# Causal attention ahead of two expert layers: VectorE makes both parts of head 1's next keys, ScalarE copies K1's probabilities and orders the row factors

## The chip, the cores and the metric

One core of a Trainium2 chip. The time is the device time of one launch in microseconds (us). The engines are TensorE (PE in the rows; PEld is its weight load), VectorE (DVE), ScalarE (ACT), GpSimd (POOL) and SyncE (SP, which issues most DMAs). Each engine works through its own queue in order, and semaphores join them.

## The reference

Three layers follow each other, all in float32:

```python
# attention: 4 batches, 8 heads, 576 positions, head size 64; blocks of 64 positions, causal by block
scores = (1 / 8) * q @ k.T
scores = where(block(row) >= block(column), scores, -1e9)
attn = exp(scores - max(scores))
x = (attn / (attn.sum(-1) + 1e-9)) @ v              # 2304 tokens x 512
# experts: each of 2304 tokens goes to one of 8 experts
e = argmax(x @ w_gate + bias[modality])
x = gate * (relu(x @ w1[e]) @ w2[e])
# last layers
h = x @ w_in                                         # 512 -> 2048
g = where(h >= 1, h, where(h <= -1, 0, (h + 1)**2 / 4))
out = g @ w_out                                      # 2048 -> 512
```

The change touches the attention alone.

## The kernel before

**Pairs and kinds.** The attention goes through 16 pairs of heads (4 batches of 4 pairs), numbered 0 to 15. In a pair the rows of the score matrix are cut into seven pieces, the kinds K0 to K6: K0 is rows 0 to 127 of both heads, K1 rows 128 to 255 of both, K2 and K3 rows 256 to 383 of head 0 and of head 1, K4 and K5 rows 384 to 511 of head 0 and of head 1, K6 the last 64 rows of both. One step does one kind, in the order K3, K1, K0, K4, K2, K6, K5 for the pairs 1 to 14 (pair 0 and pair 15 have orders of their own). Pair 3 lies at about 48 to 60 us, pair 8 at 109 to 122 us, pair 14 at 183 to 197 us.

**A step.** `scores` puts the scores of a kind into PSUM (TensorE; the last matmul, L339, adds the causal mask). `flip` turns, with TensorE, the probabilities of the kind two steps back (L378), and they are copied from PSUM into the tile pT: by ScalarE for the kinds in `ON_ACT` (L389), otherwise by VectorE, but then only behind the maximum of this step (`later`, L524). `soft` takes the maximum of each row (VectorE, L354, L358; K6 L349), and ScalarE makes the exponentials and, with a second short instruction, their sums (L360). In each step a copy on ScalarE stands ahead of the exponentials. The PSUM tiles of scores and of flips have two buffers each; those of a kind are free when its exponentials, or its copies, are done. K6 shares one buffer, two banks, with the turned q and k of the next pair.

**What hangs on the steps.** `PLAN` names what `act` issues ahead of the scores (0), behind them (1) or at the end (2) of a step. In the third step of pair n, at its end: `load_k(n + 1)` ("k"), the weighted values of pair n - 1 (`weigh`, 20 matmuls, L403), and `weigh_first` (4 matmuls, L418, and the copy into xT, L422). At the beginning of the fourth step "low" issues the low parts of the next keys, L490; in its middle the copy of the weighted values into xT, L408 ("store").

**Keys.** `load_k` turns k into the PSUM tile psk (576 columns; the upper 64 partitions are head 1, the lower head 0). VectorE copies the first 128 columns into kT (L292). ScalarE rounds each head's half into kd, 64x576 (L294, two instructions). GpSimd copies each half to the other partitions (L296). In the next step VectorE subtracts kd from psk into kl, for both heads (L490, two instructions), and with that psk is free.

**Row factors.** Behind each second pair `row_sums` inverts the sums of the exponentials (VectorE, L427, L428), and `row_order`, called by `weigh_first`, brings them into the order of the tokens: one or two copies of 16 numbers for each partition (L439) and two copies of 2 (L445), from SBUF to SBUF, on VectorE. `rows` uses them later: it multiplies with them on VectorE (L461, L465), behind matmuls on xT (L455).

In pairs 14 and 15 the first steps of the routing are put in between, up to three small VectorE groups for each step (L667 and on).

Of the kernel before, what the change touches and what calls it, by code (L numbers as in the profile page):

```python
# [11 lines left out]
F32 = mybir.dt.float32  # L12
# [6 lines left out]
ALU = mybir.AluOpType  # L19
# [7 lines left out]
B, H, S, D = 4, 8, 576, 64  # L27
NB = S // 64
NP = H // 2
# [20 lines left out]


ORDER_FIRST, ORDER_LAST, ORDER = (2, 4, 0, 1, 5, 6, 3), (3, 1, 4, 2, 6, 0, 5), (3, 1, 0, 4, 2, 6, 5)
PLAN = {(1, 0): ["rows", "q"], (2, 0): ["sum"], (2, 2): ["k", (0, 5), "first"], (3, 0): ["low"], (3, 1): ["store"],
        (4, 0): ["rows"], (6, 2): ["rows"]}
FROM = 0, 128, 256, 320, 448
LAG = 2
COPY = 4
ON_ACT = (0, 2, 3, 4, 5)


KDUP = 1, 1, 0, 0
# [61 lines left out]
def attention(late, weights, tc, q, k, v, ids, w_gate, mbias, x_dram, dram, ident, tabs):  # L123
# [3 lines left out]
    nc = tc.nc  # L127
# [54 lines left out]
    def turned(dst, x):  # L182
        if x.dtype == F32R:
            nc.tensor.transpose(dst.bitcast(F32R), x, identr)
        else:
            nc.tensor.transpose(dst, x, ident)
# [53 lines left out]
    rt = keep.tile([P, NJ, H], F32, name="rt")  # L240
# [4 lines left out]
    def load_q(n):  # L245
        psq = ps2.tile([P, 1024], F32, tag="big", name=f"psq{n}")
        psq = psq[:, 64:64 + S]
        for t, x in enumerate(FROM):
            turned(psq[:, x:x + P], io_t[n, "q"][:, t, :])
        qa, qb, qf = qas[n % 2], qbs[n % 2], qfs[n % 2]  # L250

        qT = wk.tile([P, 9, 64], F32, tag="qT", name=f"qT{n}", bufs=1)
        nc.scalar.activation(qT, psq.rearrange("p (i t) -> p i t", t=64), AF.Copy, scale=D ** -0.5)
        E = nc.gpsimd if n else nc.vector
        copy = nc.gpsimd.tensor_copy if n else nc.scalar.copy
        halves = [(h, slice(h * 64, h * 64 + 64), slice(64 - h * 64, 128 - h * 64)) for h in range(2)]
        for h, hs, oh in halves:
            copy(qa[hs, h, :7], qT[hs, 2:])
            if not n:
                E.tensor_tensor(qa[oh, h, :7], qT[hs, 2:], qa[hs, h, :7].bitcast(F32), op=ALU.subtract)  # L260
        if n:
            for h, hs, oh in halves:
                E.tensor_tensor(qa[oh, h, :7], qT[hs, 2:], qa[hs, h, :7].bitcast(F32), op=ALU.subtract)
        for h, hs, oh in halves:
            copy(qf[hs, h].rearrange("p (i t) -> p i t", t=64), qT[hs, :2])
        E.tensor_copy(qb[:64, :7], qa[:64, 0, :7])
        E.tensor_copy(qb[64:, 7], qa[64:, 1, 6])
        E.tensor_copy(qb[64:, 8:], qa[64:, 1, :6])
        nc.gpsimd.tensor_copy(qzs[n % 2][:, 64:], qa[:, 1, 6])

    low_k = {}

    def load_k(n):
        if n:
            psk = ps2.tile([P, 1024], F32, tag="big", name=f"psk{n}")[:, 64:64 + S]
            ranges = [(psk, slice(0, S))]
        else:

            pk = [ps2.tile([P, 512], F32, tag="x", name=f"psk{n}_{i}", bufs=2) for i in range(2)]
            ranges = [(pk[0][:, :448], slice(0, 448)), (pk[1][:, :P], slice(448, S))]  # L280
        for t, x in enumerate(FROM):
            if n:
                dst = psk[:, x:x + P]
            else:
                dst = pk[t // 4][:, x % 448:x % 448 + P]
            turned(dst, io_t[n, "k"][:, t, :])
        kT = wk.tile([P, S if n == 0 else P], F32, tag="kT" if n else "kT0", name=f"kT{n}", bufs=2 if n else 1)
        kd = wk.tile([P, 2, S], F32R, tag="kd", name=f"kd{n}")
        kl = wk.tile([P, S], F32R, tag="kl", name=f"kl{n}")
        halves = [(h, slice(h * 64, h * 64 + 64), slice(64 - h * 64, 128 - h * 64)) for h in range(2)]  # L290
        if n:
            nc.vector.tensor_copy(kT, psk[:, :P])  # L292
            for h, hs, oh in halves:
                nc.scalar.copy(kd[hs, h], psk[hs])  # L294
            for h, hs, oh in halves:
                nc.gpsimd.tensor_copy(kd[oh, h], kd[hs, h])  # L296
            low_k[n] = [(kl[hs], psk[hs], kd[hs, h].bitcast(F32)) for h, hs, oh in halves]
        else:
            for a, cs in ranges:
                nc.vector.tensor_copy(kT[:, cs], a)  # L300
            for h, hs, oh in halves:
                for u, dst in enumerate((kd[hs, h], kd[oh, h])):
                    if KDUP[2 * h + u] == 0:
                        for a, cs in ranges:
                            nc.scalar.copy(dst[:, cs], a[hs])
                    else:
                        nc.vector.tensor_copy(dst, kT[hs])
                nc.vector.tensor_tensor(kl[hs], kT[hs], kd[hs, h].bitcast(F32), op=ALU.subtract)
        qk[n] = kT, kd, kl
# [53 lines left out]
    def flip(n, i):  # L363
# [10 lines left out]
        for o, k0, k1 in todo:  # L374
# [10 lines left out]
            else:  # L385
                dst = pTs[n][:, :k1, heads[0], P * j:P * (j + 1)]
                src = pt[:, :m, :]
            if i in ON_ACT:
                nc.scalar.copy(dst, src)  # L389
# [16 lines left out]
    def store_xT(n):  # L406
        b, c = divmod(n, NP)
        nc.scalar.copy(xT[:, c, b % 2 * S + 64:(b % 2 + 1) * S], pxs.pop(n))  # L408

    def weigh_first(n, order=True):  # L410

        b, c = divmod(n, NP)
        if n < B * NP - 1:
            px = ps1.tile([P, 512], F32, tag="pt", name=f"py{n}", bufs=4 - SB)
        else:
            px = ps2.tile([P, 512], F32, tag="x", name=f"py{n}", bufs=2)
        for h in range(2):
            nc.tensor.matmul(px[h * 64:(h + 1) * 64, :64], io_t[n, "v"][:, 0, h * D:(h + 1) * D],  # L418
                             pTs[n][:, 0, h, :64], start=True, stop=True)
        if c % 2 and order:  # L420
            row_order(b, c // 2)
        nc.scalar.copy(xT[:, c, b % 2 * S:b % 2 * S + 64], px[:, :64])  # L422

    def row_sums(b, a):

        r = rinv[:, b, 2 * a:2 * a + 2]
        nc.vector.tensor_scalar(r, ssum[:, b, 2 * a:2 * a + 2], 1e-9, None, op0=ALU.add)  # L427
        nc.vector.reciprocal(r, r)  # L428

    def row_order(b, a):  # L430

        r = rinv[:, b, 2 * a:2 * a + 2]
        j0 = NB * b // 2
        if b % 2 == 0:
            parts = [((0, P), (0, P), j0)]
        else:
            parts = [((64, P), (0, 64), j0), ((0, 64), (64, P), j0 + 1)]
        for (lo, hi), (slo, shi), j in parts:
            nc.vector.tensor_copy(rt[lo:hi, j:j + 4, 4 * a:4 * a + 4].rearrange("p j (c h) -> p c h j", h=2),  # L439
                                  r[slo:shi, :, :8].rearrange("p c (h j) -> p c h j", h=2))  # L440

        lo, hi = 64 * (b % 2), 64 * (b % 2) + 64
        rr = rt[lo:hi, j0 + 4, 4 * a:4 * a + 4].rearrange("p (c h) -> p c h", h=2)
        for h in range(2):
            nc.vector.tensor_copy(rr[:, :, h], r[64 * h:64 * h + 64, :, 8])  # L445

    def rows(j, a, spare=False, xr=None):

# [30 lines left out]
    def act(n, z, at):  # L479

        if n >= B * NP:
            return
        for what in PLAN.get((z, at), ()):
            if what == "q" and n + 1 < B * NP:
                load_q(n + 1)
            elif what == "k" and n + 1 < B * NP:
                load_k(n + 1)
            elif what == "low" and n + 1 in low_k:
                for dst, a, b in low_k.pop(n + 1):
                    nc.vector.tensor_tensor(dst, a, b, op=ALU.subtract)  # L490
            elif what == "rows" and todo:
                done.add(todo[0])
                rows(*todo.pop(0))
            elif n == 0:
                continue
            elif isinstance(what, tuple):
                weigh(n - 1, *what)
            elif what == "sum" and (n - 1) % 2:
                row_sums((n - 1) // NP, (n - 1) % NP // 2)
            elif what == "first":  # L500
                weigh_first(n - 1)
            elif what == "store":
                store_xT(n - 1)
                if (n - 1) % 2:
                    todo.extend((j, (n - 1) % NP // 2) for j in rows_of[(n - 1) // NP])
# [5 lines left out]
    for g in range(len(steps) + LAG):  # L511
        n, z = divmod(g, NK)
# [30 lines left out]
    ps1_ctx.close()  # L543
    tail = Tables()
    tail.pv, tail.ps2 = pv_ctx, ps2_ctx
    tail.row_sums = lambda: (row_sums(B - 1, 1), row_order(B - 1, 1))
    tail.weigh = lambda: weigh(B * NP - 1, 0, 5)
    tail.store_xT = lambda: store_xT(B * NP - 1)
    tail.weigh_first = lambda: weigh_first(B * NP - 1, False)
    tail.rows, tail.left = rows, todo + [(j, 1) for j in rows_of[B - 1]]  # L550
    return tail, routing, early

# [1030 lines left out]
```

## Time and profile before

| | |
|---|---|
| runs shown | 835.45, 835.92, 838.87 us; median 835.92 |
| profiled execution | 830.86 us, span 829.1 us |
| TensorE | 806.4 us busy, 97% of the span |
| VectorE | 590.8 us, 71% |
| ScalarE | 477.1 us, 58% |
| GpSimd | 212.0 us, 26% |
| mean granted TensorE clock | 0.997 |

All views are of the one profiled execution. Busy time is the union of an engine's instructions. A matmul's end is modelled, with the time that it takes through the array, so TensorE can be shown busy while a weight load already waits; a wait shows best in the start of the next instruction. [...]

### The profile page before, as it was taken

Reading aid. Unit: us, or ns where it says so; the run is one execution under the profiler, and the core shown is the slowest. Engines: PE = TensorE matmul, PEld = TensorE weight load, DVE = VectorE, ACT = ScalarE, POOL = GpSimd, SP = SyncE. Lnnn points to the kernel's source line nnn. Section 1 sums busy time; section 2 is a strip of 40 time slices with the busy share of each in tenths; the row PEclk is TensorE's granted clock in tenths of the full one; section 3 lists DMA queues with packets and bytes.
Section 4 is the critical chain, followed back from the end, with each engine's and each line's share of the span. In section 5 each row is a group of like instructions: output and inputs, shape, how many; then the busy total and the mean of one; then the engine's idle time right before and its main releaser. Section 6 shows DMA issues by size and latency. Waiting matters only on the chain. (4 is left out here: it accounts for less than half of the span.)

```text
span 829.1 us, 13988 instructions
## 1 busy us (share of the span) xinstructions
PE 806.4 (97%) x4936; PEld 699.8 (84%) x4936; DVE 590.8 (71%) x1071; ACT 477.1 (58%) x964; POOL 212.0 (26%) x313
## 2 busy tenths in 40 slices
PE   6999999998999999999999999999999999999998
PEld 5777777776788888888888999999999988888887
DVE  6777787778756646697873766666636888887784
ACT  4877877776533335455544766766657644444442
POOL 8546556646315414140201000000000011112120
PEclk9999999999999999999999999999999999999999
DMA  7565565532736547665624553554634643333301
GB/s 158 125 163 141 143 166 160 143 81 71 248 80 124 189 135 244 221 203 168 198 87 125 179 174 127 173 176 138 218 130 155 239 149 127 128 127 126 132 35 39
DMA packets 140988, 123.21 MB, mean 149 GB/s; under 512 B 73111, under 2 KB 125351, under 8 KB 138224
## 3 DMA queue, kind: packets, MB, share of 16 engines
q1 hardware_dynamic: 134576, 107.99, 42.9%
q0 software_dynamic: 4992, 13.94, 4.8%
q8 instruction: 41, 0.67, 0.3%
q10 hardware_dynamic: 1344, 0.33, 0.2%
q14 instruction: 35, 0.29, 0.1%
HBM read 89.18 MB, written 40.38 MB: 156 GB/s over the span
## 5 line engine op out<-in xcount | busy, mean ns | idle before, releaser
L1018 PE MATMUL h<-yhi,wi 128*128 128x384 f32 x768 | 199.1, 337 | 1.1 <-ACTq L1257 1.1
L1018 PEld LDWEIGHTS h<-yhi,wi 128*128 128x128 f32 x768 | 138.9, 188 | 1.6 <-ACTq L1257 1.6
L1018 PE MATMUL h<-ylo,wi 128*128 128x384 f32 x384 | 128.7, 335 | 0.0
L1482 POOL DMA_INDIRECT out_dram<-rest,tab x16 | 27.4, 1711 | 336.5 <-DVE rest L1449 331.6
L360 ACT ACTIVATE pall<-s,nmax 128x384 f32<-128x384 f32 (+2 forms) x144 | 79.6, 562 | 35.0 <-DVE nmax L358 29.8
L1297 ACT ACTIVATE cl<-h,half 128x384 f32<-128x384 f32 x96 | 55.8, 581 | 65.1 <-PE h L1018 62.7
L1301 DVE SCALAR_TENSOR_TENSOR gg<-cl,h 128x384 f32<-128x384 f32 x96 | 52.2, 551 | 49.4 <-ACT cl L1298 48.6
L1427 PE MATMUL p<-wo,s 128*128 128x256 f32 (+1 forms) x432 | 87.0, 337 | 0.0
L1427 PEld LDWEIGHTS p<-wo,s 128*128 128x128 f32 x432 | 67.6, 188 | 9.2
L378 PE MATMUL pt<-ident,pall 128*128 128x128 f32 x400 | 65.9, 283 | 6.7 <-ACT pall L360 4.7
L1018 PEld LDWEIGHTS h<-ylo,wi 128*128 128x128 f32 x384 | 72.1, 188 | 0.0
L1427 PE MATMUL p<-wo,a 128*128 128x256 f32 (+1 forms) x330 | 65.4, 334 | 0.0
L1018 PE MATMUL h<-xhi,wh 128*128 128x512 f32 (+2 forms) x164 | 63.7, 388 | 0.0
L1018 PE MATMUL h<-xlo,wh 128*128 128x512 f32 (+2 forms) x164 | 62.1, 379 | 0.4 <-DVE xlo L76 0.4
L1018 PE MATMUL h<-xhi,wl 128*128 128x512 f32 (+2 forms) x164 | 62.2, 379 | 0.4 <-DVE wl L1104 0.2
L1129 PE MATMUL acc<-wh,hl 128*128 128x512 f32 x152 | 59.6, 392 | 0.8 <-DVE hl L1118 0.8
L1129 PE MATMUL acc<-wh,hh 128*128 128x512 f32 x152 | 59.6, 392 | 0.0
L1129 PE MATMUL acc<-wl,hh 128*128 128x512 f32 x152 | 59.4, 391 | 0.0
L1427 PEld LDWEIGHTS p<-wo,a 128*128 128x128 f32 x330 | 52.2, 188 | 8.0
L1298 ACT ACTIVATE cl<-cl 128x384 f32<-128x384 f32 x96 | 50.5, 526 | 3.0
L378 PEld LDWEIGHTS pt<-ident,pall 128*128 128x128 f32 x400 | 43.1, 142 | 10.4 <-ACT pall L360 8.3
L1101 ACT CAST wh<-raw 128x1024 fp32r<-128x1024 f32 x40 | 41.8, 1047 | 15.7 <-PE acc L1129 15.7
(312 smaller groups left out, 1774.2 us busy)
## 6 DMA issues: line engine op xcount, KB each, us to landing
raw<-in_moe_w_dram SPq DMA_DIRECT2D x80, 256.0 KB, 3.5
g_dram<-gg SPq DMA_DIRECT2D x48, 384.0 KB, 2.6
g<-g_dram SPq DMA_DIRECT2D x18, 1024.0 KB, 4.9
wi_raw<-in_moe_w_in_dram SPq DMA_DIRECT2D x16, 512.0 KB, 4.7
wo_raw<-in_moe_w_out_dram SPq DMA_DIRECT2D x16, 512.0 KB, 4.0
yr<-y_dram SPq DMA_DIRECT2D x18, 256.0 KB, 4.6
x_dram<-xrow SPq DMA_DIRECT2D x34, 128.0 KB, 2.2
v<-in_v_dram SPq DMA_DIRECT2D x32, 128.0 KB, 2.4
```

The source lines that it names most:

```text
L360: nc.scalar.activation(pall[n % 2][:, o:o + w], pss[:, u:u + w], AF.Exp, bias=nm[:, x:x + 1], scale=1.0, accum_out=ssum[:, b, c, x:x + 1])
L378: nc.tensor.transpose(pt[:, kk, :], pa[:, o + kk * P:o + (kk + 1) * P], ident)
L1018: nc.tensor.matmul(ps, a[za], b[zb], start=(i == 0), stop=(i == n - 1))
L1101: nc.scalar.copy(ws[s, f][0], weights.raw[s, f])
L1129: nc.tensor.matmul(accs[s][u], a[:, us], b[:, 1, :], start=(f == 0 and i == 0), stop=(f == NF - 1 and i == 2))
L1297: nc.scalar.activation(cl, ph, AF.Relu, bias=half, scale=0.5)
L1298: nc.scalar.activation(cl, cl, AF.Square)
L1301: nc.vector.scalar_tensor_tensor(gg[:, :, f % 2, :], cl.rearrange(t3, t=P), 1.0, ph.rearrange(t3, t=P), op0=ALU.min, op1=ALU.max)
L1427: nc.tensor.matmul(o, a, b, start=(x == 0 and i in FRESH), stop=(x == len(terms) - 1), skip_group_check=True)
L1482: outs.append(nc.gpsimd.indirect_dma_start(out=out[:, :], out_offset=bass.IndirectOffsetOnAxis(ap=tabs.tab[:, j:j + 1].bitcast(U32), axis= ...
```

## The change

There are three edits. ScalarE copies K1's probabilities too (`ON_ACT`), so of the copies only K6's stay with VectorE. `load_k` gives head 1's kd to VectorE, which makes head 1's low part right behind it, in the third step; head 0's kd stays with ScalarE, and head 0's low part stays at the beginning of the fourth step. `row_order` goes from `weigh_first` to an entry of its own, "order", ahead of "k", and runs on ScalarE; for the last pair it stays on VectorE.

```diff
-PLAN = {..., (2, 2): ["k", (0, 5), "first"], (3, 0): ["low"], ...
+PLAN = {..., (2, 2): ["order", "k", (0, 5), "first"], (3, 0): ["low"], ...
-ON_ACT = (0, 2, 3, 4, 5)
+ON_ACT = (0, 1, 2, 3, 4, 5)
@@ load_k
             nc.vector.tensor_copy(kT, psk[:, :P])
-            for h, hs, oh in halves:
-                nc.scalar.copy(kd[hs, h], psk[hs])
-            for h, hs, oh in halves:
-                nc.gpsimd.tensor_copy(kd[oh, h], kd[hs, h])
-            low_k[n] = [(kl[hs], psk[hs], kd[hs, h].bitcast(F32)) for h, hs, oh in halves]
+            low = [(kl[hs], psk[hs], kd[hs, h].bitcast(F32)) for h, hs, oh in halves]
+            for h, copy in ((1, nc.vector.tensor_copy), (0, nc.scalar.copy)):
+                copy(kd[halves[h][1], h], psk[halves[h][1]])
+                if h:
+                    nc.vector.tensor_tensor(*low[1], op=ALU.subtract)
+                nc.gpsimd.tensor_copy(kd[halves[h][2], h], kd[halves[h][1], h])
+            low_k[n] = low[:1]
@@ weigh_first
-        if c % 2 and order:
-            row_order(b, c // 2)
@@ row_order: each nc.vector.tensor_copy becomes copy
-    def row_order(b, a):
+    def row_order(b, a, copy=nc.scalar.copy):
@@ act
+            elif what == "order":
+                if (n - 1) % 2:
+                    row_order((n - 1) // NP, (n - 1) % NP // 2)
@@ the last pair
-    tail.row_sums = lambda: (row_sums(B - 1, 1), row_order(B - 1, 1))
+    tail.row_sums = lambda: (row_sums(B - 1, 1), row_order(B - 1, 1, nc.vector.tensor_copy))
```

## Rows read from the trace of the kernel before

**Rows 1.** Busy time of a stretch: stretch, length, engines (instructions), PEclk, DMA share, GB/s.
```profile
20.00:190.00 170.00, 163.59 (x1318) 126.75 (x1319) 132.78 (x282) 132.53 (x391) 96.37 (x173) 1.00 0.53 139
```

**Rows 2.** Waits, 20 to 190 us: total, times, longest.
```profile
PEld pt L378 <- ACT pall L360: 7.7, 21, 0.4
```

**Rows 3.** Timeline of pair 3, from its fourth step: start, us, what [idle before].
```profile
53.46 1.52 DVE L490 TENSOR_TENSOR kl<-psk,kd 64x576 fp32r<-64x576 f32 x2 [2.27 <-ACT kd L294]
...
53.76 0.21 ACT L422 COPY xT<-py 128x64 f32<-128x64 f32 x1 [0.34 <-PE py L418]
...
54.22 0.20 PE L339 MATMUL s<-maskk,maskq 128*128 128x64 bf16 x1
...
54.26 0.63 PE L378 MATMUL pt<-ident,pall 128*128 128x128 f32 x4
...
55.02 0.69 DVE L358 TENSOR_REDUCE nmax<-s 128x1 f32<-128x512 f32 x1
...
55.58 0.20 PE L339 MATMUL s<-maskk,maskq 128*128 128x64 bf16 x1
...
55.62 0.68 DVE L524 COPY pT<-pt 128x512 f32<-128x512 f32 x1
55.74 0.69 ACT L360 ACTIVATE pall<-s,nmax 128x512 f32<-128x512 f32 x1 [1.28 <-DVE nmax L358]
...
56.42 0.36 ACT L389 COPY pT<-pt 128x256 f32<-128x256 f32 x1
...
56.66 0.60 PE L378 MATMUL pt<-ident,pall 128*128 128x128 f32 x4
...
56.77 0.55 DVE L358 TENSOR_REDUCE nmax<-s 128x1 f32<-128x384 f32 x1
...
57.35 0.58 ACT L360 ACTIVATE pall<-s,nmax 128x384 f32<-128x384 f32 x1 [0.57 <-DVE nmax L358]
...
57.58 0.20 PE L339 MATMUL s<-maskk,maskq 128*128 128x64 bf16 x1
...
58.08 0.31 PEld L378 LDWEIGHTS pt<-ident,pall 128*128 128x128 f32 x3 [0.41 <-ACT pall L360]
...
58.39 0.75 ACT L360 ACTIVATE pall<-s,nmax 128x576 f32<-128x576 f32 x1
...
59.28 0.53 PEld L378 LDWEIGHTS pt<-ident,pall 128*128 128x128 f32 x5 [0.37 <-ACT pall L360]
```

**Rows 4.** Timeline of pair 8, third and fourth step.
```profile
111.47 2.33 POOL L263 TENSOR_TENSOR qa<-qT,qa 64x448 fp32r<-64x448 f32 x2
...
111.60 0.29 DVE L292 COPY kT<-psk 128x128 f32<-128x128 f32 x1 [0.21 <-PE psk L184]
...
111.92 1.92 DVE L439 COPY rt<-rinv 64x16 f32<-64x16 f32 x2
...
112.83 1.29 ACT L294 CAST kd<-psk 64x576 fp32r<-64x576 f32 x2
...
115.90 0.69 DVE L358 TENSOR_REDUCE nmax<-s 128x1 f32<-128x512 f32 x1
```

**Rows 5.** Two lines' own views: duration in ns (shortest/median/longest), first and last start.
```profile
L439 DVE COPY rt<-rinv x12: 174/720/1161, 38.9 to 212.2; 64x16 f32<-64x16 f32 x8, 128x16 f32<-128x16 f32 x4
...
L389 ACT COPY pT<-pt x80: 361/485/587, 16.0 to 212.0; 128x384 f32<-128x384 f32 x32, 128x512 f32<-128x512 f32 x32, 128x256 f32<-128x256 f32 x16
```

**Rows 6.** Pairs 0 and 14: timelines, and the stretch with the lower clock as in rows 1.
```profile
20.04 0.37 PE L326 MATMUL s<-kd,qa 128*128 128x288 f32 x1 [1.79 <-DVE kl L490]
...
188.81 0.28 DVE L292 COPY kT<-psk 128x128 f32<-128x128 f32 x1
...
190.89 0.54 PE L687 MATMUL rkp<-oh,ones 128*128 128x104 bf16 x13 [1.60 <-ACT xT L422]
...
193.54 0.69 PE L378 MATMUL pt<-ident,pall 128*128 128x128 f32 x2 [1.09 <-DVE pT L524]
...
193.00:197.00 4.00, 3.46 (x16) 3.18 (x17) 3.43 (x14) 2.18 (x6) 0.07 (x1) 0.57 0.11 37
```

More of the change, by code (lines that the diff above doesn't have):

```diff
@@ L52 @@
 ORDER_FIRST, ORDER_LAST, ORDER = (2, 4, 0, 1, 5, 6, 3), (3, 1, 4, 2, 6, 0, 5), (3, 1, 0, 4, 2, 6, 5)
-PLAN = {(1, 0): ["rows", "q"], (2, 0): ["sum"], (2, 2): ["k", (0, 5), "first"], (3, 0): ["low"], (3, 1): ["store"],
+PLAN = {(1, 0): ["rows", "q"], (2, 0): ["sum"], (2, 2): ["order", "k", (0, 5), "first"], (3, 0): ["low"], (3, 1): ["store"],
         (4, 0): ["rows"], (6, 2): ["rows"]}
@@ L408, in store_xT, with weigh_first @@
         nc.scalar.copy(xT[:, c, b % 2 * S + 64:(b % 2 + 1) * S], pxs.pop(n))
-    def weigh_first(n, order=True):
+    def weigh_first(n):
         b, c = divmod(n, NP)
@@ L438, in row_order @@
         for (lo, hi), (slo, shi), j in parts:
-            nc.vector.tensor_copy(rt[lo:hi, j:j + 4, 4 * a:4 * a + 4].rearrange("p j (c h) -> p c h j", h=2),
+            copy(rt[lo:hi, j:j + 4, 4 * a:4 * a + 4].rearrange("p j (c h) -> p c h j", h=2),
                                   r[slo:shi, :, :8].rearrange("p c (h j) -> p c h j", h=2))
@@ L444, in row_order @@
         for h in range(2):
-            nc.vector.tensor_copy(rr[:, :, h], r[64 * h:64 * h + 64, :, 8])
+            copy(rr[:, :, h], r[64 * h:64 * h + 64, :, 8])
     def rows(j, a, spare=False, xr=None):
@@ L545, in attention @@
     tail.pv, tail.ps2 = pv_ctx, ps2_ctx
-    tail.row_sums = lambda: (row_sums(B - 1, 1), row_order(B - 1, 1))
+    tail.row_sums = lambda: (row_sums(B - 1, 1), row_order(B - 1, 1, nc.vector.tensor_copy))
     tail.weigh = lambda: weigh(B * NP - 1, 0, 5)
     tail.store_xT = lambda: store_xT(B * NP - 1)
-    tail.weigh_first = lambda: weigh_first(B * NP - 1, False)
+    tail.weigh_first = lambda: weigh_first(B * NP - 1)
     tail.rows, tail.left = rows, todo + [(j, 1) for j in rows_of[B - 1]]
```

## The prediction

> **What bounds the kernel now.** I read the busy time first. Over the span TensorE is busy for 97%, and in the steady part of the attention for 163.59 of 170 us [rows 1]. So time is won only where TensorE stands still, by this view 6.4 us of that stretch. Then the waits: in that stretch TensorE's weight loads for the flips wait 21 times for ScalarE's exponentials, 7.7 us [rows 2]. No other wait of TensorE there repeats.
>
> Then the order in time, for head pair 3 [rows 3]. VectorE stands still 2.27 us for ScalarE's kd copies, and only then makes the two low parts (1.52 us). The maximum of K4 is behind them in its queue and starts at 55.02, though K4's scores had ended at 54.42 (54.22 + 0.20). ScalarE waits 1.28 us for that maximum. VectorE then copies K1's probabilities (0.68) and forms the products of `rows`, so K2's maximum starts at 56.77, and ScalarE waits again, 0.57. Its exponential of K2 begins at 57.35 and TensorE, which wants to flip it behind the mask of 57.58, waits to 58.08. An unhindered flip follows its mask by 0.04 (54.22 to 54.26), so this one costs 0.46, though 0.41 is shown: each shown wait hides about 0.05. A second wait, 0.37, is for K6's exponential, which starts at 58.39 because ScalarE has run without a pause since 57.35. The reader is to see that VectorE is late by about 0.6 to 1 us in each pair, because it idles ahead of that while ScalarE does both kd copies.
>
> **The change part by part.** *Keys.* ScalarE loses one kd copy, 0.64 (1.29 for two [rows 4]). VectorE gains a copy of 64x576 out of PSUM. That row does not exist. From below: 0.29 for the 128x128 one [rows 4]; from above: the subtraction of the same size, 0.76 [rows 3]. The copy of 512 columns takes 0.68 [rows 3], so I take 0.75. It and head 1's subtraction (0.76) fit into the 2.27 us of idling, and head 0's subtraction needs ScalarE's single copy, which is done 0.64 earlier. In pair 3 VectorE would start at 51.2 (53.46 less 2.27), have head 1 done by 52.7, head 0 by 53.5, before K4's scores end at 54.42. K4's maximum starts at 54.46 instead of 55.02. The cover is the TensorE work of `weigh`; without it the copy would cost its 0.75. GpSimd's copies come in the same order, with an input that is ready earlier. No DMA moves.
>
> *K1's copy.* VectorE loses 0.68; ScalarE gains 0.58 [rows 5], ahead of K4's exponential and behind flips that end at 54.89 (54.26 + 0.63). So K4's exponential starts at 55.5 at the latest instead of 55.74: a smaller step than VectorE's. K2's maximum starts when its own scores are done (55.58 + 0.20), near 55.85 instead of 56.77, and ends near 56.4. ScalarE reaches K2's exponential 0.68 after K4's (55.74 to 56.42, the copy) and 0.36 more for that copy, at 56.5. That is 0.85 ahead of 57.35, against a wait of 0.46: the first wait goes, with 0.4 to spare. For K6: TensorE's flips of K4 end near 57.3, ScalarE's copy of them takes 0.5, the exponential 0.75, so it ends near 58.5; TensorE gets there at 58.4 (59.28 less both waits). Of the second wait about 0.15 stays.
>
> *Row factors.* In seven of the pairs VectorE loses four (or three) tiny copies: 1.92 us for the first two in pair 8 [rows 4], beside 0.17 for the shortest of these [rows 5]. They start at 111.92 and end with GpSimd's subtractions (111.47 + 2.33), so they stood still for GpSimd. On ScalarE such a copy has no row. From below 0.17, VectorE's shortest [rows 5]; the nearest row, ScalarE's 64 columns, is 0.21 [rows 3]; from above VectorE's longest, 1.16 [rows 5]. I take 0.21, four make 0.84. They stand ahead of ScalarE's kd copy: 112.83 + 0.84 + 0.64 = 114.31, head 0's subtraction ends at 115.1, and K4's maximum starts near 115.15 instead of 115.90, just when K4's scores are done. What waits behind them on ScalarE is the kd copy and the two xT copies; the first of these needs TensorE's result at 114.46 anyway. So they cost nothing, with 0.2 to spare.
>
> [...]
>
> *The sum.* Pairs 1 to 13: of the 21 waits three (0.9) belong to pair 0, which I keep apart. 18 are left, 6.8 shown and 0.9 hidden, 7.7 in all. From this I take 0.15 for each of the five pairs with a second wait: 7.0. Pair 0: TensorE waits 1.79 for the low part of pair 1's keys [rows 6]; the subtraction ends 0.75 earlier, but K1's copy then lies in a stretch in which ScalarE is full, so between 0 and 0.8, and I take 0.5. [...] VectorE now goes from its key copy at 188.81 to the end of the K1 copy, which releases TensorE at 193.5; with 0.28 + 0.75 + 0.76, a short wait for kd, 0.76 and 0.69 it would be done at 192.2, so 1.2 us earlier. [...] I take 1.8, between 1.0 and 2.9. Sum: 7.0 + 0.5 + 1.8 = 9.3 us.
>
> The profiled execution took 830.86 us (829.1 of span and 1.8 around it), 5.1 below the median of 835.92. So 821.6 by its own measure, and carried to the median **826.6 us**. Nothing behind the attention pays it back: TensorE has its work ready there, and the rest moves up as a whole.
>
> **Rivals.**
> (B) *ScalarE becomes the bound.* For it: it has run without a pause from 57.35 on, and gains 0.58 while it loses 0.64 at another place. Against it: the copy falls into its 1.28 us of waiting. If K2's exponential moves only as far as K4's, by 0.24, the 18 waits give 4.3, pair 0 nothing and pair 14 1.0: 5.3 us, 830.6.
> (C) *VectorE's copy does not run beside GpSimd*, and the change so doesn't do what it says. For it: the row factors stood still until GpSimd's subtractions were over. If the copy too started only then (in the last pairs about 2 us later), head 0's low part would end 0.3 after the one of before, and only the K1 copy that has gone would help: 1 to 3 us, 834. Against it: the key copy, also out of PSUM, started 0.13 us after GpSimd and took 0.29 [rows 4].
> [...]
> (D) *Slower: the row factors on ScalarE.* If one takes p there, K4's maximum of such a pair starts at 114.3 + 4p instead of 115.90; from p = 0.40 on the pair loses. At 1.16 (rows 5) it loses 3.0, seven pairs 21, against some 5 won elsewhere: 852. The whole kernel loses from p = 0.58. Against it: the small ScalarE copy out of PSUM takes 0.21 [rows 3].
> (E) *The clock.* If pair 14's first wait stays (ScalarE now has four small copies ahead of it and one kd copy less, 0.2 more in all) and the clock falls as before, 1.7 of the sum goes: 827.5 to 828.5, inside the range.
>
> **How the numbers follow.** The forecast, with E, 0.74; B 0.14; C 0.08; D 0.04. About 0.5% (4.2 us) is what a measurement of this kernel can tell from no change. The forecast and two thirds of B are faster; C and the rest of B, and a small part of the forecast, are the same; D is slower: 0.82, 0.14, 0.04. Range: from the upper ends (all waits 8.7, pair 0 0.8, pair 14 2.9, and 1 for the step in pair 8 that I left out: 13.4) 822.5, to B and a little beyond, 832.5.
>
> **What would show it.** Right: K4's maximum starts within 0.1 us of its scores' mask; VectorE's wait for kd is gone or under 0.2; the flips' waits fall from 7.7 to under 2; ScalarE's row factors take about 0.2 each; pair 14's second wait is gone and the clock with it stays at 1.00. Wrong: the flips still wait 4 us or more for exponentials, now behind K1's copy (B); VectorE's kd copy starts with the end of GpSimd's subtractions (C); row factors of over 0.4 (D). The forecast fails if the attention stretch is not at least 6 us shorter.

## The result and the profile after

| | before | after |
|---|---|---|
| median of the runs on one chip | 835.68 us | 828.29 us (828.16 to 828.78) |
| ratio | | 0.9906, interval 0.9879 to 0.9933 |
| profiled execution: span | 829.1 us | 827.0 us |
| the same pair on a second chip (e5 below) | 831.59 us | 826.20 us, ratio 0.9926, 0.9905 to 0.9948 |

The change makes the kernel faster by 5.4 to 7.4 us; the forecast was 826.6, within 822.5 to 832.5. It was 1.7 us too low. Two of its terms came out smaller, pair 0 and pair 14, and pair 15 lost time for which it had no term. In the profiles after, `load_k`'s copies are L295, head 1's low part L297, head 0's L490; many other lines move by 2 or 3.

First the busy time of the stretch of [rows 1], then the wait of [rows 2], in the trace after:

```profile
20.00:190.00 170.00, 165.88 (x1352) 130.03 (x1353) 129.42 (x271) 141.72 (x424) 97.72 (x175) 0.99 0.54 139
```

```profile
PEld pt L380 <- ACT pall L362: 2.3, 9, 0.3
```

TensorE stands still 4.1 us in place of 6.4 and starts 34 matmuls more (1352 against 1318), and the flips' waits for exponentials fall from 7.7 us (21 times) to 2.3 (9 times). Pair 3, beside [rows 3] (start, us, what [idle before]):

```profile
51.66 0.76 DVE L295 CAST kd<-psk 64x576 fp32r<-64x576 f32 x1
52.45 0.76 DVE L297 TENSOR_TENSOR kl<-psk,kd 64x576 fp32r<-64x576 f32 x1
53.30 0.63 ACT L295 CAST kd<-psk 64x576 fp32r<-64x576 f32 x1 [0.59 <-DVE kl L297]
53.96 0.75 DVE L490 TENSOR_TENSOR kl<-psk,kd 64x576 fp32r<-64x576 f32 x1 [0.75 <-ACT kd L295]
54.66 0.20 PE L341 MATMUL s<-maskk,maskq 128*128 128x64 bf16 x1
54.90 0.69 DVE L360 TENSOR_REDUCE nmax<-s 128x1 f32<-128x512 f32 x1 [0.18 <-PE s L341]
55.37 0.59 ACT L391 COPY pT<-pt 128x512 f32<-128x512 f32 x1 [0.47 <-PE pt L380]
56.30 0.55 DVE L360 TENSOR_REDUCE nmax<-s 128x1 f32<-128x384 f32 x1
56.88 0.58 ACT L362 ACTIVATE pall<-s,nmax 128x384 f32<-128x384 f32 x1
58.01 0.20 PE L341 MATMUL s<-maskk,maskq 128*128 128x64 bf16 x1
58.05 0.53 PE L380 MATMUL pt<-ident,pall 128*128 128x128 f32 x3
...
59.11 0.53 PEld L380 LDWEIGHTS pt<-ident,pall 128*128 128x128 f32 x5 [0.25 <-ACT pall L362]
```

K4's maximum starts 0.04 us behind its scores (54.66 + 0.20 to 54.90); before it was 0.60. K2's exponential starts 0.47 earlier, although TensorE is 0.44 later here than before (mask at 54.66 against 54.22), and its flip follows the mask at once (58.05 behind 58.01). The second wait stays. New is the third row: ScalarE's kd copy does not run beside VectorE, it starts when VectorE's subtraction has ended (52.45 + 0.76 = 53.21), and VectorE then idles 0.75 us for it.

Pair 8, beside [rows 4], and the row factors by line, beside [rows 5] (shortest/median/longest in ns):

```profile
109.21 2.33 POOL L263 TENSOR_TENSOR qa<-qT,qa 64x448 fp32r<-64x448 f32 x2
109.60 0.76 DVE L295 CAST kd<-psk 64x576 fp32r<-64x576 f32 x1
110.39 0.76 DVE L297 TENSOR_TENSOR kl<-psk,kd 64x576 fp32r<-64x576 f32 x1
110.66 0.45 ACT L439 COPY rt<-rinv 64x16 f32<-64x16 f32 x2
111.12 0.39 ACT L445 COPY rt<-rinv 64x2 f32<-64x2 f32 x2
111.54 0.63 ACT L295 CAST kd<-psk 64x576 fp32r<-64x576 f32 x1
112.20 0.75 DVE L490 TENSOR_TENSOR kl<-psk,kd 64x576 fp32r<-64x576 f32 x1 [1.05 <-ACT kd L295]
112.60 0.20 PE L341 MATMUL s<-maskk,maskq 128*128 128x64 bf16 x1
112.88 0.67 DVE L360 TENSOR_REDUCE nmax<-s 128x1 f32<-128x512 f32 x1
```

```profile
L445 ACT COPY rt<-rinv x14: 189/192/210, 40.6 to 184.2; 64x2 f32<-64x2 f32 x14
L439 ACT COPY rt<-rinv x10: 215/220/252, 40.5 to 183.8; 64x16 f32<-64x16 f32 x6, 128x16 f32<-128x16 f32 x4
```

VectorE's copy and subtraction run inside GpSimd's 2.33 us, 0.76 each. Four row factors take 0.84 us on ScalarE, and K4's maximum comes 0.08 behind its scores. Pair 14, beside [rows 6], and the clock there (columns as in rows 1):

```profile
184.00 0.76 DVE L297 TENSOR_TENSOR kl<-psk,kd 64x576 fp32r<-64x576 f32 x1
184.85 0.63 ACT L295 CAST kd<-psk 64x576 fp32r<-64x576 f32 x1 [0.47 <-DVE kl L297]
185.38 0.20 ACT L422 COPY xT<-py 128x64 f32<-128x64 f32 x1
185.64 0.79 PE L690 MATMUL rkp<-oh,ones 128*128 128x104 bf16 x13 [2.17 <-ACT xT L422]
```

```profile
182.00:186.00 4.00, 1.83 (x23) 1.31 (x20) 3.15 (x9) 2.77 (x12) 2.85 (x7) 0.93 0.00 0
186.00:190.00 4.00, 4.00 (x32) 3.69 (x30) 3.09 (x11) 2.28 (x7) 0.21 (x1) 0.65 0.10 35
```

The held kd copy holds the xT copy, TensorE stands 2.17 us (before 1.60), and the granted clock, a share of the full one, is 0.65 in the next 4 us: 0.50 up to 188.8 us, 1.00 behind that. The wait for VectorE's copy of K1, 1.09 us before, is gone.

Both kernels run the same 4936 matmuls in one order, so the start of each can be compared: before minus other kernel, in us, what each stretch gave (times of before; the stretch names the pairs; the wait at 20.04 us in [rows 6] lies ahead of the first one):

| | 20–34 pair 0 | 34–183 pairs 1–13 | 183–205 pair 14 | 205–255 pair 15 | 255–300 experts |
|---|---|---|---|---|---|
| after | 0.0 | 6.6 | 0.7 | −0.9 | −3.6 |
| e1 keys alone | 0.5 | 6.3 | 0.1 | −3.0 | 0 |
| e2 K1 alone | −0.4 | 6.4 | 1.5 | 0.1 | 0 |
| e3 order alone | 0.0 | −3.3 | −1.6 | −0.1 | 0 |
| e4 keys and K1 | 0.0 | 6.6 | 1.8 | −0.6 | 0 |
| e5 after, again | 0.0 | 6.6 | 0.6 | −2.4 | 0 |
| e6 both kd on VectorE | 0.0 | 6.6 | 1.7 | −0.3 | 0 |
| e7 row factors twice | 0.0 | 5.7 | 0.0 | −0.2 | 0 |
| e8 e4 and both kd | 0.0 | 4.8 | 0.2 | −0.3 | 0 |
| e9 issue order | −1.0 | 6.1 | 1.0 | −0.9 | −2.1 |
| e10 e6, K1 in pair 0 | 0.4 | 6.6 | 1.7 | −1.2 | −2.2 |
| e11 e6, again | 0.0 | 6.6 | 1.7 | −0.9 | −2.9 |

Ahead of 20 us the kernels differ by up to 0.8 us, but two executions of one kernel do too (after −0.8, e5 +0.1).

### The profile page after: what moved, and what is told of

It is laid out like the page before. It is cut to its first block, busy times and chain, and to the rows that moved or that the text cites. A ratio compares the mean times of both kernels' runs of the same rounds, so it can differ in the third digit from the quotient of the medians.

```text
span 827.0 us, 14008 instructions
## 1 busy us (share of the span) xinstructions
PE 805.5 (97%) x4936; PEld 699.1 (85%) x4936; DVE 581.7 (70%) x1046; ACT 482.1 (58%) x989; POOL 212.7 (26%) x313
## 5 line engine op out<-in xcount | busy, mean ns | idle before, releaser
L391 ACT COPY pT<-pt 128x384 f32<-128x384 f32 (+2 forms) x96 | 49.4, 515 | 17.3 <-PE pt L380 16.6
```

## Experiments: the parts one by one

My theory: the steady gain is one wait in each pair, TensorE's for K2's exponential, and it goes as soon as VectorE reaches K2's maximum 0.5 us earlier, by whichever part; so the parts don't add. The rival: each has its own share.

**e1, keys alone.** Only the edit of `load_k`; `ON_ACT` and `row_order` as before.

> The keys' part alone: VectorE makes head 1's kd copy and low part first; K1's copy stays on VectorE, the row factors stay on VectorE in their old place. My theory (the gain is that VectorE's lateness ahead of K2's maximum goes, and the flips then no longer wait for the exponential): K4's maximum starts 0.5 us earlier, K2's maximum with it, which covers the 0.46 of the first wait; so this part alone gives most of the whole, 829 to 831 us against 828.3 for both parts and 835.7 before; the flips' waits from 20 to 190 us fall from 7.7 to under 3.5. Rival (each part takes its own share, and the shares add up): 831.5 to 833, flips' waits 4 to 5 us.

Measured: 824.90 against 830.87 (this chip's kernel before is faster), ratio 0.9919 (0.9900 to 0.9939). The flips wait 2.1 us, under the 3.5 expected. In pair 3 (trace of e1) K4's maximum is on time and K1's copy, still on VectorE, fits in between:

```profile
53.57 0.20 PE L341 MATMUL s<-maskk,maskq 128*128 128x64 bf16 x1
53.81 0.69 DVE L360 TENSOR_REDUCE nmax<-s 128x1 f32<-128x512 f32 x1 [0.18 <-PE s L341]
54.42 0.68 DVE L526 COPY pT<-pt 128x512 f32<-128x512 f32 x1
55.45 0.55 DVE L360 TENSOR_REDUCE nmax<-s 128x1 f32<-128x384 f32 x1
56.03 0.58 ACT L362 ACTIVATE pall<-s,nmax 128x384 f32<-128x384 f32 x1 [0.24 <-DVE nmax L360]
```

**e2, K1's copy alone.**

```diff
-ON_ACT = (0, 2, 3, 4, 5)
+ON_ACT = (0, 1, 2, 3, 4, 5)
```

> K1's copy alone goes to ScalarE; keys and row factors as before. My theory: K4's maximum stays late (55.0 in pair 3), but VectorE is rid of 0.68 between it and K2's maximum, so K2's exponential can start some 0.5 us earlier unless ScalarE is held by K1's copy (0.58) ahead of K4's exponential; that copy lies in ScalarE's wait of 1.28 us. So this part alone too gives most: 829 to 831.5 us, and the two parts don't add up. Rival (shares add up): 831.5 to 833. Second rival (ScalarE's own load decides, since it gains 0.58 here and loses nothing): 834 to 837, with the flips' waits at 7 us or more.

Measured: 823.73, ratio 0.9913 (0.9897 to 0.9930); the flips wait 3.6 us. K4's maximum stays 0.59 late (mask at 54.58, maximum at 55.37), but K2's exponential is ready all the same.

**e3, the row factors alone.** `PLAN`'s "order" and ScalarE's copies; `load_k` and `ON_ACT` as before.

> The row factors alone go to ScalarE and to the third step's start; keys and K1's copy as before. My theory: the copies stood in VectorE's queue in seven pairs for 1.9 us, but ahead of a K4 maximum that is late by the low parts anyway; each costs ScalarE 0.84 us ahead of its two kd copies, which are here still the ones that VectorE waits for. So 834.5 to 837.5, no gain worth telling. Rival (they are part of the gain): 833 to 834.

Measured: 835.88, ratio 1.0063 (1.0046 to 1.0081): slower by 5.0 us, and my expectation missed it. Pair 8 (trace of e3):

```profile
114.68 0.45 ACT L437 COPY rt<-rinv 64x16 f32<-64x16 f32 x2
115.56 1.29 ACT L294 CAST kd<-psk 64x576 fp32r<-64x576 f32 x2
116.62 0.20 PE L339 MATMUL s<-maskk,maskq 128*128 128x64 bf16 x1
116.88 1.52 DVE L488 TENSOR_TENSOR kl<-psk,kd 64x576 fp32r<-64x576 f32 x2 [3.29 <-ACT kd L294]
```

On VectorE the copies lay in its wait for kd and made the low parts at most 0.2 us later (pairs 6 and 8); on ScalarE they stand ahead of both kd copies. The subtractions start when K4's scores are done, and TensorE loses 0.85 us in each of the pairs 6 and 8, which have four copies (0.84), and about 0.4 in those with three; the flips wait 10.6 us.

**e4, keys and K1**, the row factors on VectorE in their old place.

> Keys and K1's copy as in the changed kernel, the row factors on VectorE in their old place. My theory: in the seven pairs with row factors VectorE's copies stand still for GpSimd's subtractions, up to 1.1 us each, and K4's maximum starts later by 1 to 2 us in some of them; K1's copy no longer follows, so VectorE catches up in part. 828.5 to 831 us, 0 to 2.5 slower than the changed kernel. Rival (the row factors on ScalarE cost time, as in pair 14 where they stand ahead of kd): 827 to 828.

Measured: 823.88, ratio 0.9917 (0.9898 to 0.9936). So the three gains of pairs 1 to 13 are 6.3, 6.4 and, together, 6.6: my theory holds, shares don't add. The row factors' place is worth nothing there (6.6 with either). In pair 14 e4 gives 1.8 against 0.7 and 0.6 in the changed kernel's two traces, but TensorE's wait at rkp is the same (trace of e4; 2.17 with the row factors on ScalarE):

```profile
185.65 0.54 PE L689 MATMUL rkp<-oh,ones 128*128 128x104 bf16 x13 [2.16 <-ACT xT L424]
```

```profile
186.00:190.00 4.00, 4.00 (x40) 3.57 (x36) 3.93 (x16) 3.41 (x9) 0.35 (x2) 1.00 0.11 37
```

What differs is the clock: 1.00 from 186 to 190 us. In e1, which has the row factors on VectorE too, the wait is 2.18 and the clock there falls to 0.58. So it is not shown that the row factors' place on ScalarE costs anything in pair 14. The expectation, a later maximum of K4 behind VectorE's copies, isn't borne out, and its rival isn't either: by the ratio e4 lies between the changed kernel's two (0.9906 and 0.9926).

## Experiments: ScalarE's held copy

**e5, the changed kernel** once more.

> The changed kernel itself, unaltered, beside the others on one chip. In the first profile of it TensorE lost 3.5 us from 266 to 280 us, behind a ScalarE cast that came late, while the attention ahead of it was 5.6 us shorter. My theory: that loss is an execution's own (it shows in no profile of the four part-kernels) and belongs to no part of the change; so without it the changed kernel stands at about 0.993 of the kernel before here, 1.3 us behind the one with keys and K1 alone (0.9917), because in pair 14 its row factors on ScalarE cost 1.3. Rival: the loss belongs to the changed order of work and shows again: ratio 0.996 to 0.998.

Measured: 826.20 against 831.59, ratio 0.9926 (0.9905 to 0.9948), the number that was expected; its reason, a cost of the row factors in pair 14, is not shown (e4). The 3.6 us of the experts don't appear. But pair 15 loses 2.4 us, at a granted clock of 0.57 from 206 to 210 us:

```profile
202.00:206.00 4.00, 2.33 (x18) 1.77 (x17) 3.09 (x11) 3.63 (x12) 1.89 (x2) 1.00 1.06 381
206.00:210.00 4.00, 4.00 (x14) 1.54 (x16) 1.83 (x2) 0.81 (x2) 1.58 (x1) 0.57 0.48 160
```

The loss starts at one matmul, which waits for the DMA that gathers the tokens of the first experts (first row, e5); in the kernel before it stood half as long, for ScalarE (second row):

```profile
PE xt L1097 <- DMA xg<-x_dram,gidx: 1.3, 1, 1.3
```

```profile
PE xt L1094 <- ACT pT L389: 0.6, 1, 0.6
```

In e1, which loses 3.0, the same wait is 2.2 us. The ten traces with the edit of the keys lose 0.2 to 3.0 us in pair 15, those of e2, e3 and e12 without it nothing (0.1 either way), though e2 comes there as early. From GpSimd's issue to its landing the gather takes 6.3 us in e5, 5.6 before and 5.3 in e2; why it differs stays open. So does the clock: in e4 TensorE is busy 2.71 us from 202 to 206, and the clock is 1.00 behind it.

**e6, both kd copies on VectorE.**

```diff
-            for h, copy in ((1, nc.vector.tensor_copy), (0, nc.scalar.copy)):
+            for h, copy in ((1, nc.vector.tensor_copy), (0, nc.vector.tensor_copy)):
```

> The changed kernel with head 0's kd copy on VectorE too (ScalarE makes none after pair 0). My theory: ScalarE's copy starts only when VectorE's subtraction for head 1 has ended, because both read the same PSUM tile and the second engine's read is held behind the first's; in pair 14 that holds ScalarE's xT copy and with it TensorE for 2.17 us, and the clock falls. With the copy on VectorE the xT copy starts about 0.9 us earlier, the wait is 1.0 to 1.4, and the row factors (0.84) still stand ahead of it: 0.8 to 1.6 us faster than the changed kernel, K4's maximum no later in the steady pairs (VectorE's copy 0.76 against ScalarE's 0.63 with its two handovers). Rival (TensorE waits in pair 14 for something else, or VectorE becomes the bound): same or up to 2 us slower.

Measured: 823.14, ratio 0.9902 (0.9886 to 0.9918). Pair 14 (trace of e6):

```profile
183.55 0.39 ACT L445 COPY rt<-rinv 64x2 f32<-64x2 f32 x2
183.97 0.21 ACT L422 COPY xT<-py 128x64 f32<-128x64 f32 x1
184.23 0.54 PE L690 MATMUL rkp<-oh,ones 128*128 128x104 bf16 x13 [1.23 <-ACT xT L422]
```

The wait is 1.23 us, inside 1.0 to 1.4 and now behind the row factors, the clock stays at 1.00, and the pair gives 1.7. In the traces of e10 and e11, which have the same edit, it is 1.22 and 1.24, and the pair gives 1.7 again. The steady pairs lose nothing: four operations on VectorE in a row take as long as three with two handovers (in pair 3 of e6 and of the changed kernel 3.1 us behind the kT copy). The medians differ by 3.1 us; the two traces differ by 3.2, most of it in pair 15, where this one lost 0.3 and e5's 2.4.

**e8, e4 with both kd copies on VectorE.**

> Keys and K1 as in the changed kernel, the row factors on VectorE in their old place, and head 0's kd copy on VectorE too. [...] 1 to 2 us faster than keys and K1 alone: 0.989 to 0.991 of the kernel before. Rival (VectorE's chain of two copies, two subtractions and the row factors makes K4's maximum late again): 0.992 to 0.995.

Measured: 825.80, ratio 0.9935 (0.9917 to 0.9952): the rival. The wait at rkp fell to 0.21, but the row factors stand between VectorE's copies and its last subtraction, and TensorE waits for that:

```profile
187.46 0.34 DVE L447 COPY rt<-rinv 64x2 f32<-64x2 f32 x2
187.83 0.75 DVE L492 TENSOR_TENSOR kl<-psk,kd 64x576 fp32r<-64x576 f32 x1
188.63 0.40 PE L328 MATMUL s<-kd,qa 128*128 128x288 f32 x1 [1.99 <-DVE kl L492]
```

So with all of the keys on VectorE the row factors belong on ScalarE: worth 3.3 us by the traces (6.6 + 1.7 of e6 against 4.8 + 0.2).

**e7, the row factors twice.**

```diff
-                    row_order((n - 1) // NP, (n - 1) % NP // 2)
+                    for _ in range(2):
+                        row_order((n - 1) // NP, (n - 1) % NP // 2)
```

> The changed kernel with the row factors written twice on ScalarE (the second time the same values), 0.84 us more ahead of the kd copy in six pairs, in pair 14 too. My forecast put their cost at nothing with 0.2 us to spare. By that, 0.6 us of the 0.84 is exposed at K4's maximum, but VectorE without K1's copy has about 0.4 in hand ahead of K2's exponential: 0.2 to 0.3 in each of six pairs and 0.8 to 1.5 in pair 14, so 2 to 3.5 us slower than the changed kernel. Rival (ScalarE's time counts in full): 0.84 each, 5 to 6 us slower, as the row factors alone cost about 5 without the other two parts. Second rival (much slack): under 1 us.

Measured: 825.94, ratio 0.9930 (0.9915 to 0.9944), the same as the changed kernel beside it, so by the time the expectation missed. The trace shows the dose: 0.4 and 0.5 us less in the pairs 6 and 8, where it is four copies (0.84), nothing in those with three, and 0.6 less in pair 14, 1.5 in all against the 2 to 3.5 expected; in this trace pair 15 lost 2.2 less than in e5's, which hides it. In pair 8 K4's maximum is 1.0 late (mask at 112.95 and 0.20, maximum at 114.18), so the room of 0.2 that I saw at K4's maximum wasn't there; the one behind it, ahead of K2's exponential, takes up half.

**e9, the issue order.** All operations as in the changed kernel; GpSimd's two copies too are issued behind the subtraction:

```diff
             for h, copy in ((1, nc.vector.tensor_copy), (0, nc.scalar.copy)):
                 copy(kd[halves[h][1], h], psk[halves[h][1]])
-                if h:
-                    nc.vector.tensor_tensor(*low[1], op=ALU.subtract)
+            nc.vector.tensor_tensor(*low[1], op=ALU.subtract)
+            for h in (1, 0):
                 nc.gpsimd.tensor_copy(kd[halves[h][2], h], kd[halves[h][1], h])
```

> The changed kernel with one line moved: VectorE's subtraction for head 1 is issued behind ScalarE's kd copy of head 0, no longer ahead of it; all operations are the same. My theory (two engines' reads of one PSUM tile are held in the order in which they are issued): ScalarE's copy then starts at the end of VectorE's kd copy, 0.8 us earlier in pair 3, and VectorE's subtraction, which started 0.03 behind its kd copy, now waits for ScalarE, 0.6 to 0.8 us, though it reads nothing that ScalarE writes. The chain to head 0's subtraction keeps its length where ScalarE is free and grows by up to 0.4 where the row factors stand ahead; TensorE's wait at the routing step in pair 14 falls from 2.17 to 1.6 to 1.8. Time: within 1.5 us of the changed kernel. Rival (the copy of head 0 waited for VectorE for another reason): the subtraction still follows its kd copy by under 0.1 us, and both run side by side; then 0.5 to 1.5 us faster.

Measured: 831.69 against 837.13, ratio 0.9946 (0.9925 to 0.9967). No changed kernel ran on this chip; by the ratio e9 is 1.7 us slower than e5, with intervals that overlap. Its trace loses 1.0 in pair 0, where the clock is 0.50 from 22 to 24 us and the changed kernel's 1.00. Pair 3 (trace of e9, ScalarE's and VectorE's rows):

```profile
52.37 0.64 ACT L295 CAST kd<-psk 64x576 fp32r<-64x576 f32 x1
```

```profile
51.46 0.76 DVE L295 CAST kd<-psk 64x576 fp32r<-64x576 f32 x1
53.04 0.76 DVE L296 TENSOR_TENSOR kl<-psk,kd 64x576 fp32r<-64x576 f32 x1 [0.82 <-ACT kd L295]
```

Now the hold is on the other side: VectorE's subtraction for head 1 waits for ScalarE's copy of head 0, of which it reads nothing, in all 15 pairs. The wait at rkp is 1.73. So in both kernels the engine whose read of psk is issued later waits for the other's: ScalarE 5.9 us (12 times) in the changed kernel, VectorE 15.9 us (15 times) in e9. In the changed kernel the wait is for a semaphore: ScalarE's queue has one ahead of each of its 15 copies (L295). The two engines share the tile kd as well, but that is not what holds them: in the changed kernel GpSimd's copy of head 1's half, issued between the two, reads and writes kd too, and in pair 3 ScalarE's copy doesn't wait for it (53.30, against this row of the changed kernel):

```profile
55.81 1.39 POOL L298 CAST kd<-kd 64x576 fp32r<-64x576 f32 x2
```

In the kernel before no time is shown lost by the hold: ScalarE idles ahead of none of its 30 kd copies. The two heads lie on partitions 0 to 63 and 64 to 127; whether two reads that share no partition need the hold, no run here shows.

**e10, K1 on VectorE in pair 0**, on top of e6, and **e11, e6 again** as its neighbour.

```diff
-            if i in ON_ACT:
+            if i in ON_ACT and (n or i != 1):
```

> Both kd copies on VectorE as in the fastest kernel so far, and in pair 0 alone K1's copy on VectorE as before the change. My theory: in pair 0 ScalarE is the late engine, and K1's copy there cost TensorE about 0.3 us between 20 and 34 us; the same comes back, 0.2 to 0.5 us, at the edge of what can be measured (ratio to the kernel before 0.9895 to 0.9902, against 0.9902); in the trace the step from 20 to 34 us is 0.25 to 0.4 us shorter. Rival: nothing, since VectorE is then the late one there.

> The kernel with both kd copies on VectorE once more, on this chip, so that the one with pair 0 altered has its neighbour and the gain over the changed kernel is seen twice. 0.989 to 0.991 of the kernel before; if the first result was an execution's luck, 0.992 to 0.994.

Measured: 827.56 and 828.23, ratios 0.9912 (0.9878 to 0.9946) and 0.9912 (0.9881 to 0.9943). The traces show pair 0's 0.4 us as expected, the times can't. e6's gain over the kernel before came a second time, just outside the expected 0.989 to 0.991.

**e12, the kernel before** with a second profile.

> The kernel before, unaltered, once more with a profile. The time of the kernel before differs between chips (830.9 and 831.6 on two, 835.7 and 837.1 on two others), and on the latter two the traces of changed kernels lose 2.1 to 3.6 us between 266 and 280 us, behind a cast on ScalarE; the one trace of the kernel before that exists, 830.86, loses nothing there. My theory: where the time of the kernel before is 834 or more, its trace has that loss too, at the same instructions; where it is 830 to 832, not. Rival: the loss occurs in changed kernels alone, and then the change costs time on such chips that its ratio already holds.

Measured: 830.17 against 831.12 of itself, ratio 0.9989 (0.9973 to 1.0006). Its trace follows the first one within 0.5 us throughout and loses nothing among the experts. It ran on a chip of 831, so the theory's other half, that the kernel before loses time there on the slower chips, was not tested.

## Why the prediction was right, and where it failed

- *What bounds the kernel.* Right: VectorE's lateness ahead of K2's maximum, removed once in each pair. Pairs 1 to 13 give 6.6 against a forecast of 7.0. The second wait, of which I left 0.15, keeps 0.31 in pair 3 (59.11 behind 58.76, where an unhindered flip follows by 0.04). I priced the two edits as one chain, which they are, but didn't see that each alone was enough (e1, e2): e2, one number more in `ON_ACT`, has the ratio 0.9913, the whole change 0.9906 and 0.9926.
- *Keys.* VectorE's copy takes 0.76 (taken: 0.75) and runs beside GpSimd, so rival C is out. The step of the sum that failed is "head 0's subtraction needs ScalarE's single copy, which is done 0.64 earlier": that copy is held behind VectorE's subtraction (e9), VectorE still idles 11.9 us for it (15 times), and head 0 is done at 54.71 in pair 3, or 54.27 by TensorE's time of before, not at 53.5. So the two copies and two subtractions still follow one another: from the end of the kT copy to the end of the last low part they take 3.1 us in the traces after (3.4 in pairs 6 and 8, behind four row factors). In the kernel before they took 3.6 to 4.0 in pairs 1 to 13, where ScalarE began 0.8 to 0.9 us behind kT (in pair 8 at 112.83, behind 111.60 + 0.29 [rows 4]), but 3.1 in pairs 0 and 14, where it began 0.2 behind kT. In pair 14 of the kernel before, behind 188.81 + 0.28 [rows 6]:

```profile
189.33 1.28 ACT L294 CAST kd<-psk 64x576 fp32r<-64x576 f32 x2
```

What this part takes away is ScalarE's lateness in pairs 1 to 13; in pairs 0 and 14 it made nothing shorter.

- *K1's copy.* Right: the first wait is gone. ScalarE got fuller (132.53 to 141.72 us) without becoming the bound, so B is out. K2's maximum came at 56.30, 55.86 by TensorE's time of before (forecast: near 55.85).
- *Row factors.* The price was right (0.21 taken; 0.215 to 0.252 and 0.189 to 0.210 measured), so D is out. "They cost nothing" was right for pairs 1 to 13 (after against e4), and in pair 14 no cost is shown while the copy of head 0 is held; "with 0.2 to spare" was wrong (e7).
- *Pair 14, the mis-sized term.* Taken 1.8, measured 0.7 and 0.6: in number rival E, whose 1.7 is 4 us less 0.57 of them [rows 6]. No run of the changed kernel shows the 1.8: 1.2 of it is VectorE's shorter way from 188.81 to 193.5, the rest was an estimate for a clock that stays at 1.00, and its two traces show 0.65 and 0.57 from 186 to 190 us. The second wait went, as forecast, and gave 1.2; but the first wait rose by 0.57 (1.60 to 2.17) and the clock fell. What raised the wait is the held copy, not the four small copies that E names: it is 2.16 with the row factors on VectorE (e4), 1.23 without the hold (e6) and 0.21 without either (e8). With only the held copy taken away the clock stayed at 1.00 there in three of three traces (e6, e10, e11) and the pair gave 1.7. With the hold the clock fell in both traces of the changed kernel and in e1, e7 and e9 (0.58, 0.77 and 0.63 from 186 to 190 us), but not in e4 (1.00); what decides that stays open.
- *Pair 0.* Taken 0.5, measured 0. The step that failed is "the subtraction ends 0.75 earlier": the chain of the keys is as long as before there, and the wait of 1.79 us is 1.79 in e1 and 1.78 in e5. (It is 1.38 in the first trace after, where TensorE came 1.2 us later.) Behind it the keys give 0.5 (e1), and K1's copy on ScalarE takes 0.4 back (e2, e10 against e11).
- *The signs.* K4's maximum (0.04 and 0.08 us behind its scores) and the row factors' 0.2 came as named. The flips' waits fell to 2.3, not under 2; VectorE's wait for kd stayed; pair 14's second wait went, but the clock didn't stay at 1.00.
- *"Nothing behind the attention pays it back."* Wrong in part. Pair 15 lost 0.9 and 2.4 us in the changed kernel's two traces. So my own mark, an attention at least 6 us shorter, was met by the first trace only if counted from 20 us (6.5 from 20 to 255 us, 5.6 from the start), and missed by the second (4.8 and 4.9). Then in the first trace 3.6 us went among the experts, where TensorE is busy 3.95 us of 6 in place of 6.00, behind a cast on ScalarE of the weights in `raw`. The view names no instruction of this core that ended its wait (remote), so that it waits for the weights' DMA is argued:

```profile
262.00:268.00 6.00, 3.95 (x18) 2.96 (x17) 0.00 (x0) 0.00 (x0) 2.83 (x3) 1.00 0.82 262
```

```profile
268.05 1.05 ACT L1104 CAST wh<-raw 128x1024 fp32r<-128x1024 f32 x1 [10.86 <-remote]
```

Among the changed kernels that loss goes with the chip: the traces of e9, e10 and e11, from a chip where the kernel before takes 837.1, lose 2.1 to 2.9 at this place, and the nine traces of e1 to e8 and e12, from chips of 830.9 to 831.6, lose nothing. That the kernel before loses it too on such chips is argued from its time alone. Its first profiled execution, 830.86, was 4.8 us under the median of 835.68 and is none of the runs listed; the record names no chip for it, and it fits the chips of 830.9 to 831.6. So the forecast's step from 821.6 to 826.6 may rest on a difference between chips.

With the terms as measured in e5 (6.6 + 0.0 + 0.6 less 2.4, and 0.3 in the rest) the kernel gains 5.1 us by the traces and 5.4 by the medians, of 9.3 forecast. That the first measurement came as near as 1.7 us is in part luck: its medians give 7.4 us, more than the terms as measured in its trace add up to (6.6 + 0.0 + 0.7 less 0.9 is 6.4, before the 3.6 among the experts).

The lowest ratio of the study is e6's: 0.9902, and 0.9912 on a second chip (e11), 3.1 us ahead of the changed kernel on the same chip. The intervals overlap (0.9886 to 0.9918 against 0.9905 to 0.9948).

## What to carry to other kernels

Where one engine is late at one point for two reasons, taking either away can remove the whole wait behind it; run each part alone before you pay for both: here one number more in `ON_ACT` gave about as much as the whole change. When you give two halves of a PSUM tile to two engines, look at which of the two reads is issued first: they may follow each other with handovers, and one engine doing both can be as fast (3.1 us either way). Here the split shortened the chain only by the time by which ScalarE had been late. An operation moved to another engine is free only in the stages where that engine has room ahead of what others wait for: the row factors cost nothing in pairs 1 to 13 beside the other two parts, and alone they cost 5.0 us.

## What the runs showed of the hardware

A copy of 16 numbers for each partition from SBUF to SBUF took VectorE 0.17 us alone (the shortest of [rows 5], in pair 15), but 0.65 to 1.16 where GpSimd's subtractions ran; on ScalarE, beside the same subtractions, it took 0.217 to 0.252. VectorE's 64x576 copy out of PSUM took 0.76 in all 15 pairs beside GpSimd's work. The granted clock fell behind the same wait of TensorE in some executions and not in others (2.18 us: 0.58 in e1; 2.16 us: 1.00 in e4). The kernel before had medians of 830.9, 831.6, 831.1 and 837.1 us on four chips and 835.7 in the first measurement, so times of different measurements are compared by ratio only.
